# Reordering the start-up loads of a convolution and feed-forward kernel: weights by need, an ungated weight load, and one input held back

**The chip, the cores and the metric.** The kernel runs on one core of a Trainium2 chip. Times are device microseconds of that core, as medians of several executions of one build. The kernel before took 700.02 us when the prediction was made (three runs, 699.57 to 701.13).

## The reference, cut to what matters

```python
# x: [8, 4096, 192] f32, weight: [8 heads, 7] f32, w_in: [192, 2048], w_out: [2048, 192]
w   = softmax(weight, axis=-1)                    # 7 taps for each head of 24 channels
x_pad = concatenate([zeros(6 rows), x], axis=1)
y   = sum over k of w[h, k] * x_pad[:, s + k, h*24:(h+1)*24]    # causal depthwise convolution
h   = y.reshape(32768, 192) @ w_in
g   = maximum(0.01 * h, h)
out = g @ w_out                                   # [32768, 192] f32
```

## The kernel before

TensorE does both matrix products in bf16. VectorE does most of the convolution with one multiply and six multiply-adds for each chunk of 64 channels. ScalarE evicts the first product with the leaky ReLU. Two batch rows are worked on together, one in partitions 0 to 63 and one in 64 to 127, so `w_in` is needed in both halves of the partitions ("both rows"). The first blocks are cut in halves of 256 positions, to start early. A group is one such half. Group 0 has eight units; each unit is two 128-column tiles of `w_in`, twelve matmuls and one ScalarE activation of about 1 us.

Everything that the change touches is in the first 30 us. Four quarters of `w_in` are loaded with a cast on the way (f32 to bf16, from the GpSimd queue). Quarter 0 goes to both rows from HBM. Quarters 1 to 3 go to one row, and the sync queue copies them to the other on chip:

```python
    load_w_in(0, 0)
    load_w_in(0, 1)
    ...                                    # softmax, taps, first transposes
    for q in range(1, WQ):
        load_w_in(q, 0)                    # GpSimd queue, HBM -> row 0
    ...                                    # taps as diagonal matrices for TensorE
    for q in range(1, WQ):                 # sync queue, row 0 -> row 1
        nc.sync.dma_start(out=w_in[CH:128, :, fq[q]], in_=w_in[0:CH, :, fq[q]])
    load_first(2)                          # x of half 2, sync queue

    pjunk = const_pool.tile([1, 1], BF16)  # the gate: GpSimd reads the last w_in element
    nc.gpsimd.tensor_copy(out=pjunk, in_=w_in[0:1, NCH - 1, F - 1 : F])
    w_out = const_pool.tile([128, NFC, D], BF16)
    nc.gpsimd.dma_start(out=w_out, in_=moe_w_out.rearrange("(c p) d -> p c d", p=128))
    ...
    for job in conv_jobs(groups[0], range(NPEC, NCH)):
        job()
    load_first(3)                          # x of half 3, sync queue
```

In group 0 (i is the group, u the unit, j the step of two units):

```python
                mm1(grp, u)                                    # 12 matmuls and the activation
                if i == 0 and u == 3:
                    for job in pe_ahead: job()                 # convolution of half 1, on TensorE
                if i == 1 and u in (0, 2):
                    cast_first(3, u // 2, nc.scalar.copy)      # half 3 to bf16, on ScalarE
            ...
            if i == 0 and j == 3:                              # after unit 7
                ...
                for e in range(2): cast_first(2, e, nc.vector.tensor_copy)
                transpose_first(2)                             # on TensorE
                evac_first(2, nc.vector.tensor_copy, nc.vector.tensor_copy)
            ...
            if i == 1 and j == 1:
                transpose_first(3)
```

## Time and profile before

"Idle before" is the time in which TensorE stood still in front of a group of matmuls. The name behind it is what ended the wait. GpSimd's loads run on the software queue (q0 in the profile) and the sync engine's on the hardware queue (q1).

| Kernel before, profiled run | us |
|---|---|
| Span, TensorE busy | 698.4, 688.0 |
| Copies of w_in quarters 1, 2, 3: issued | 11.85, 12.86, 13.79 |
| The same: landed | 14.67, 15.66, 17.28 |
| w_out: issued, landed | 14.21, 25.45 |
| TensorE idle before unit 2 (copied w_in) | 0.91 |
| TensorE idle before half 2's transposes (x) | 1.63 |
| TensorE idle before the first use of w_out | 0.73 |
| VectorE starts half 2's convolution | 24.14 |
| TensorE meets VectorE at the first full block, and waits | 120.47, 0.62 |

### The profile page before, as it was taken

What the parts mean: (1) busy time and instruction counts of PE and PEld (TensorE: products, weight loads), DVE (VectorE), ACT (ScalarE), POOL (GpSimd) and SP (SyncE); (2) the same over time, 40 slices, a digit from 0 to 9 for tenths busy, and PEclk for the clock granted to TensorE, in tenths of its full rate; (3) what the DMA queues carried; (4) which work ended last, traced back from release to release, by engine and by line L of the source; (5) the groups of instructions that cost most, each with busy time, mean ns of one, the idle gap of its engine ahead of it and who ended that gap; (6) DMA issues with size and microseconds to landing.
All of it is one profiled execution on the core that took longest, in us unless ns stands there. A gap on an engine that the chain in (4) does not pass through costs nothing.

```text
span 698.4 us, 25999 instructions
## 1 busy us (share of the span) xinstructions
PE 688.0 (99%) x11756; PEld 610.6 (87%) x11756; DVE 542.8 (78%) x998; ACT 511.6 (73%) x571; POOL 142.3 (20%) x198
## 2 busy tenths in 40 slices
PE   8899999999999999999999999999999999999997
PEld 6799999678888888888888888888888888888887
DVE  7799999967777787777787777787777787777712
ACT  5778887977777777777777777777777777777770
POOL 4632220410222210222211222210222211000000
PEclk9999999999999999999999999999999999999999
DMA  7979544755565645556635556634556625122112
GB/s 149 131 91 101 83 71 81 80 77 79 73 74 86 85 66 75 77 74 86 86 65 81 73 74 84 88 69 74 75 74 84 89 63 77 54 52 60 45 36 70
DMA packets 184848, 54.39 MB, mean 78 GB/s; under 512 B 148384, under 2 KB 184736, under 8 KB 184736
## 3 DMA queue, kind: packets, MB, share of 16 engines
q0 software_dynamic: 98144, 13.58, 28.8%
q1 hardware_dynamic: 86592, 39.15, 23.5%
q8 instruction: 92, 1.51, 0.9%
q14 instruction: 20, 0.16, 0.1%
HBM read 28.70 MB, written 25.17 MB: 77 GB/s over the span
## 4 chain that ended last, share of the span: by engine, by line
PE 82%; DVE 13%; DMA 2%; issue 1%; POOL 1%; SPq 0%; ACT 0%; POOLq 0%; ACTq 0%
PE po L385 42%; PE ph L365 40%; DVE yt L174 12%; DMA w_in<-in_moe_w_in_dram 1%; DMA x_nat<-in_x_dram 1%; DVE yt L168 1%; POOL w_in L231 0%; DVE xt L149 0%; POOL sel L220 0%; ACT g L372 0%; SPq L319 0%; SPq L110 0%; DVE x_bf L120 0%; PE ptr L135 0%; POOL sel L218 0%
## 5 line engine op out<-in xcount | busy, mean ns | idle before, releaser
L372 ACT ACTIVATE g<-ph 128x1024 bf16<-128x1024 f32 x512 | 496.5, 1021 | 165.1 <-PE ph L365 165.1
L174 DVE SCALAR_TENSOR_TENSOR yt<-xt,wk,yt 128x512 bf16<-128x512 bf16 (+1 forms) x648 | 442.6, 683 | 17.7
L385 PE MATMUL po<-w_out,g 64*128 64x192 bf16 (+1 forms) x8048 | 398.2, 243 | 0.7 <-DMA w_out<-in_moe_w_out_dram 0.7
L385 PEld LDWEIGHTS <-g 64*128 64x128 bf16 (+1 forms) x8048 | 372.5, 94 | 29.5 <-issue 1.1
L365 PE MATMUL ph<-yt,w_in 64*128 64x512 bf16 (+1 forms) x3552 | 392.4, 347 | 3.0 <-ACT g L372 0.9
L365 PEld LDWEIGHTS <-w_in 64*128 64x128 bf16 x3552 | 249.9, 94 | 48.2 <-issue 5.1
L79 POOL DMA_DIRECT2D x_bf<-in_x_dram x180 | 133.7, 768 | 421.5 <-DMA xt<-x_bf 418.9
L424 DVE COPY o_sb<-po 128x192 f32<-128x192 f32 x216 | 77.3, 358 | 127.0 <-PE po L385 124.7
L168 DVE TENSOR_SCALAR yt<-xt,wk 128x512 bf16<-128x512 bf16 (+1 forms) x108 | 38.2, 353 | 0.1
L424 ACT COPY o_sb<-po 128x192 f32<-128x192 f32 x40 | 13.0, 325 | 0.0
L193 PE MATMUL acc<-xt,diag 64*64 64x256 bf16 x84 | 5.5, 282 | 0.0
L244 PE MATMUL warm<-zero 128*128 128x256 bf16 x18 | 4.3, 400 | 1.1 <-DVE junk L210 1.1
L193 PEld LDWEIGHTS <-diag 64*64 64x64 bf16 x84 | 4.5, 112 | 1.0 <-issue 0.6
L120 DVE CAST x_bf<-x_nat 128x384 bf16<-128x384 f32 x3 | 1.3, 424 | 4.8 <-DMA x_nat<-in_x_dram 4.8
L120 ACT CAST x_bf<-x_nat 128x384 bf16<-128x384 f32 x5 | 2.5, 506 | 1.9 <-DMA x_nat<-in_x_dram 1.9
L244 PEld LDWEIGHTS <-zero 128*128 128x128 bf16 x18 | 2.0, 131 | 1.9 <-DVE junk L210 1.1
L135 PEld LDWEIGHTS <-x_bf 64*128 64x128 bf16 x48 | 1.1, 101 | 2.6 <-DVE x_bf L120 1.9
L231 POOL DMA_DIRECT2D w_in<-in_moe_w_in_dram x5 | 3.3, 657 | 0.0
L135 PE MATMUL ptr<-ident,x_bf 64*128 64x64 bf16 x48 | 1.6, 202 | 1.6 <-DVE x_bf L120 1.6
L149 DVE COPY xt<-ptr 128x384 bf16<-128x384 bf16 x7 | 2.2, 352 | 0.4 <-PE ptr L135 0.4
L328 ACT ACTIVATE yt<-acc,rsum 128x256 bf16<-128x256 f32 x2 | 0.9, 474 | 1.9 <-PE acc L193 1.8
L296 ACT ACTIVATE diag<-ident,wkl 128x64 bf16<-128x64 bf16 x7 | 1.9, 339 | 0.0
(31 smaller groups left out, 14.4 us busy)
## 6 DMA issues: line engine op xcount, KB each, us to landing
out_dram<-o_sb SPq DMA_DIRECT2D x128, 192.0 KB, 2.1
x_bf<-in_x_dram POOLq DMA_DIRECT2D x180, 64.0 KB, 3.2
x_nat<-in_x_dram SPq DMA_DIRECT2D x8, 192.0 KB, 5.5
xt<-x_bf SPq DMA_TRANSPOSE x90, 2.5
w_in<-in_moe_w_in_dram POOLq DMA_DIRECT2D x5, 192.0 KB, 7.5
w_out<-in_moe_w_out_dram POOLq DMA_DIRECT2D x1, 768.0 KB, 11.2
w_in<-w_in SPq DMA_DIRECT2D x3, 192.0 KB, 2.8
w<-in_weight_dram SPq DMA_DIRECT2D x1, 0.2 KB
```

The costliest lines, as they stand in the source:

```text
L79: nc.gpsimd.dma_start(out=t[:, c, :, e, :], in_=src[2 * rp + e, :, :, c * CH : (c + 1) * CH],)
L120: copy(out=x_bf[q // 2][:, :, h * HS : (h + 1) * HS, e, :], in_=x_nat[q][:, e, :, :].rearrange("p s (c k) -> p c s k", c=NCH),)
L135: nc.tensor.transpose(out=ts[i][:, s, c, :], in_=x_bf[q // 2][ps, c, (q % 2) * HS + s, :, :].rearrange("p e k -> p (e k)"), identity=ident ...
L168: lambda s=src, d=dst, c=c: nc.vector.tensor_scalar_mul(d, s, wk[:, c, 0:1])
L174: lambda s=src, d=dst, c=c, k=k: nc.vector.scalar_tensor_tensor(out=d, in0=s, scalar=wk[:, c, k : k + 1], in1=d, op0=mybir.AluOpType.mult, ...
L193: lambda k=k, p=p, a=a, e=e, ps=ps: nc.tensor.matmul(out=acc[ps, :T], lhsT=diag[c][ps, p, k, :], rhs=xt[0][ps, c, a : a + T], start=(k == ...
L231: nc.gpsimd.dma_start(out=w_in[e * CH : (e + 1) * CH, :, fq[q]], in_=moe_w_in[:, fq[q]].rearrange("(c p) f -> p c f", p=CH),)
L244: nc.tensor.matmul(out=wa[:, 0, 0:HT], lhsT=zero[:, 0:128], rhs=zero, start=True, stop=True)
L365: nc.tensor.matmul(out=ph[:, e, i * T : (i + 1) * T], lhsT=w_in[ps, c, f * 128 : (f + 1) * 128], rhs=y[ps, c, t0 : t0 + T], start=(c == 0) ...
L372: act = nc.scalar.activation(out=g[blk][:, nf * u : nf * (u + 1), :, t0 : t0 + T], in_=ph.rearrange("p e (i t) -> p i e t", i=nf), func=my ...
L385: ins = nc.tensor.matmul(out=po[m], lhsT=g[b][ps, fc, e, s * 128 : (s + 1) * 128], rhs=w_out[ps, fc, :], start=(rt != 1 and fc == 0), stop ...
L424: copy(out=o_sb[:, n % 2, :], in_=po.pop(n))
```

## The change

The intent is to have each load arrive in the order in which it is needed. It has three parts.

* **Order.** Both rows of the first two quarters come from HBM, and only quarters 2 and 3 are copied on chip.
* **Ungated.** `w_out` is issued without waiting for `w_in`.
* **Hold.** x of half 3 is not issued until unit 5 of group 0 has been activated. Its casts and transposes move two units later.

A fourth, small item comes with it: the transposes of half 1 move behind both start-up convolutions, and two warming matmuls go.

```diff
-    def load_first(q):
+    def load_first(q, after=None):
 ...
+            if after is not None and e == 0:
+                tc.add_manual_dep(ins.ins, after.ins.name, ...)     # cut
 ...
-    for q in range(1, WQ):
+    load_w_in(1, 0)
+    load_w_in(1, 1)
+    for q in range(2, WQ):
         load_w_in(q, 0)
 ...
-    for q in range(1, WQ):
+    for q in range(2, WQ):
         nc.sync.dma_start(out=w_in[CH:128, :, fq[q]], in_=w_in[0:CH, :, fq[q]])
     load_first(2)
-
-    pjunk = const_pool.tile([1, 1], BF16)
-    nc.gpsimd.tensor_copy(out=pjunk, in_=w_in[0:1, NCH - 1, F - 1 : F])
     nc.gpsimd.dma_start(out=w_out, in_=moe_w_out.rearrange("(c p) d -> p c d", p=128))
 ...
-    load_first(3)
 ...                                       # transposes of half 1 after both convolutions
-                mm1(grp, u)
+                act = mm1(grp, u)
 ...
-                if i == 1 and u in (0, 2):
-                    cast_first(3, u // 2, nc.scalar.copy)
+                if i == 0 and u == 5:
+                    load_first(3, act)
+                if i == 1 and u in (4, 5):
+                    cast_first(3, u - 4, nc.scalar.copy)
 ...
-            if i == 1 and j == 1:
+            if i == 1 and j == 2:
                 transpose_first(3)
```

## The prediction

> **What bounds the kernel now.** I read the page first, then the chain that ended last, then the timeline of TensorE over the first 30 us, and last the DMA queues over short windows. From the page:
>
> ```profile
> PE 688.0 (99%) x11756; PEld 610.6 (87%) x11756; DVE 542.8 (78%) x998; ACT 511.6 (73%) x571; POOL 142.3 (20%) x198
> ...
> PE 82%; DVE 13%; DMA 2%; issue 1%; POOL 1%; SPq 0%; ACT 0%; POOLq 0%; ACTq 0%
> ```
>
> TensorE is busy for 688.0 of 698.4 us. The change only reorders loads at the start and adds no arithmetic, so all it can touch is part of the 10.4 us in which TensorE stands still. The whole of it would be 1.5% of the span. What can be won is decided by the chain, here its early part (start us, length us, what):
>
> ```profile
> 5.53 8.25 DMA w_in<-in_moe_w_in_dram
> ...
> 13.79 0.59 SPq L319
> ...
> 15.08 7.51 DMA x_nat<-in_x_dram
> ...
> 22.62 0.44 DVE x_bf L120
> ...
> 23.10 0.39 PE ptr L135 x12
> 23.50 0.62 DVE xt L149 x2
> ...
> 24.14 0.55 DVE yt L168
> ```
>
> The last w_in load lands at 13.78, the sync queue issues the third on-chip copy, then x of half 2. Its second part takes 7.51 us to land, is cast, transposed and evicted, and at 24.14 VectorE starts the convolution of half 2. From there the chain is VectorE alone until it hands over:
>
> ```profile
> 119.66 0.76 DVE yt L174
> ...
> 120.47 1.04 PE ph L365 x8
> ```
>
> So there are two clocks in the start. VectorE runs without a wait from 24.14 to 120.4. TensorE runs without one from 25.49 to 119.85, and there waits 0.62 us for VectorE. The end therefore moves by the smaller of two amounts: how much earlier VectorE starts half 2, and how much earlier TensorE gets into its steady flow plus 0.62. After 124 us TensorE has no wait longer than the issue gaps, so what is won by then is kept.
>
> TensorE in the start (the idle time before a group and its releaser in brackets):
>
> ```profile
> 11.70 1.38 PE L365 MATMUL ph<-yt,w_in 64*128 64x256 bf16 x22 [0.35 <-ACT yt L328]
> 13.53 0.27 PE L365 MATMUL ph<-yt,w_in 64*128 64x256 bf16 x1 [0.46 <-ACT g L372]
> 14.71 1.48 PE L365 MATMUL ph<-yt,w_in 64*128 64x256 bf16 x23 [0.91 <-DMA w_in<-w_in]
> 16.12 1.72 PE L193 MATMUL acc<-xt,diag 64*64 64x256 bf16 x28
> ...
> 19.72 1.75 PE L365 MATMUL ph<-yt,w_in 64*128 64x256 bf16 x24 [0.46 <-ACT g L372]
> 23.10 0.35 PE L135 MATMUL ptr<-ident,x_bf 64*128 64x64 bf16 x12 [1.63 <-DVE x_bf L120]
> ...
> 25.49 1.31 PE L385 MATMUL po<-w_out,g 64*128 64x192 bf16 x14 [0.73 <-DMA w_out<-in_moe_w_out_dram]
> ```
>
> The three DMA waits are what the change aims at: 0.91 us for the copied rows of w_in's second quarter, 1.63 for x of half 2, 0.73 for w_out. Together they are 3.3 us.
>
> **What the Trainium skill says.** "DMA: Bandwidth & Descriptors", section "Queues, rings and completion order", says that each DMA engine alternates between the queues it has work for, a packet at a time. That would give the sync queue its turn beside w_out. The trace agrees only late. Two windows of the DMA view, 18 to 20 us and then 21 to 23 us (packets, MB, share):
>
> ```profile
> q0 software_dynamic: 773, 0.30, 128.6%
> q1 hardware_dynamic: 68, 0.05, 10.3%
> ```
> ```profile
> q0 software_dynamic: 456, 0.17, 69.8%
> q1 hardware_dynamic: 416, 0.30, 61.3%
> ```
>
> In the first 3 us of w_out (from 17.0) x_nat on q1 nearly starves; from about 20.5 the two share about evenly, some 210 packets per us each. "Issuing engines are not separate DMA queues" on the same page says that all DMAs run on the same 16 engines; the starving shows that. "SBUF — State Buffer", section "SBUF: two separate sides", says that GpSimd and the faster modes of VectorE hold one port pair exclusively. The trace fits, on VectorE:
>
> ```profile
> 11.34 0.28 DVE L168 TENSOR_SCALAR yt<-xt,wk 128x256 bf16<-128x256 bf16 x1
> ...
> 14.66 0.80 DVE L168 TENSOR_SCALAR yt<-xt,wk 128x256 bf16<-128x256 bf16 x1
> ```
>
> The second one ended at 15.46, just after GpSimd's 1.22 us of w_out issue (14.21 to 15.43).
>
> **The change part by part.**
> (1) Second quarter of w_in. The five w_in loads are issued from 2.90 at 0.63 us each; the sync queue's waits put the landings of loads 3, 4 and 5 at 11.84, 12.86 and 13.78, so one lands about every 0.95 us. The new order has six: both rows of quarters 0 and 1, then one row of 2 and of 3. Quarter 1 is then whole at load 4, 12.9, where the copy landed at 14.67. But load 5 (quarter 2) comes at 13.8 and load 6 (quarter 3) at 14.7, each 0.95 later than now.
> (2) w_out. GpSimd no longer waits until 13.83. It issues the sixth load to 6.8, multiplies diag for 1.39 to 8.2, and issues w_out to 9.4. On one queue it flows behind w_in from about 13.3, instead of from 17.0. Its 2048 packets run alone at 390 per us until the copies start at about 15.3 (800 packets), and the rest at about 220: done near 20.8, against 25.4. First use is near 23, so the 0.73 wait goes. The price is that the copies and x of half 2 now run beside it.
> (3) The copies. Two, issued at 13.8 and 14.7. They took 2.8 us from issue to landing when alone and 3.5 for the third. At half the rate I take 3.8 to 4.5: quarter 2 at 17.6, quarter 3 at 19.2.
> (4) x of half 2 is issued at 15.4 and 15.9 (now 14.58 and 15.08). 512 packets of the sync queue follow the copies' 384; at about 200 per us and from 15.3 on that is 4.5 us with w_out, plus up to 1.5 for the slowest engine: second part down at 21.3, against 22.60. Half 3's 512 packets, in between now, are gone from here.
> (5) TensorE. The two warming matmuls and the transposes of half 1 leave the place between the two convolutions, so the second runs from 8.8 to 10.5 rather than 9.41 to 11.13, and ScalarE evicts it at 11.0 instead of 11.6. Work of group 0: units 0 and 1 end near 12.5 (13.1 now), units 2 and 3 start at 13.0 with quarter 1 and end at 14.4 (16.1), the convolution of half 1 runs to 16.1 (17.8). Then units 4 and 5 wait for quarter 2 until 17.6: a new wait of 1.5 us that eats most of this lead. They end at 19.0, ScalarE (0.97 us a unit) frees their buffers at 19.3 and 20.3, units 6 and 7 end at 21.0 (21.47).
> (6) So x of half 2 decides: 21.3, plus the cast to 21.75, transposes to 22.15, evictions to 22.8. VectorE starts half 2 at 22.8 rather than 24.14: 1.35 us earlier. TensorE's flow starts at 22.15 instead of 23.29 and without the 0.73: 1.9 us earlier, and the 0.62 on top. The smaller is 1.35.
> (7) Half 3 held until unit 5's activation (20.3): issued from 20.3, data from 22. The reads for block 2, issued after unit 7's activation near 22, push it aside only from 23.7. Its casts move two units later, to about 28, so I expect no wait.
> Sum: 700.0 - 1.35 = 698.6 us.
>
> **The rivals.** (a) All three waits go and nothing replaces them: TensorE ends group 0 near 20.2 and half 2's x is down by 20. VectorE would start near 21.8, a gain of 2.4, 697.6 us. For it: DMA has idle room around 12 to 13 us (28% share in the trace), which w_out would fill. Against it: the queue is near full from 15 to 23 anyway.
> (b) w_out starves the copies as it starves x_nat now (68 packets in 2 us). Quarter 2 would land at 19.5 or later, units 6 and 7 end at 22.8, VectorE starts at 24: a gain of 0.2 or a loss of up to 1, 699.8 to 701. For it: the first 3 us of w_out in the trace. Against it: output stores issued at 35 us, in the middle of a long flow on q0, land in 4.1 us, against 2.1 in the median, which is a halving and no starving.
> (c) The earlier GpSimd work (multiply and w_out issue, 6.8 to 9.4) holds VectorE's first TENSOR_SCALAR at 6.7. It would end at up to 9.4 instead of 7.64, unit 0 at 13.1, group 0's first half 0.7 later than now. The wait for quarter 2 hides that: no change of the time.
> (d) Half 3's x comes too late, ScalarE stands at the cast and holds TensorE's buffers. Over 1.1 us of it would cost time.
>
> **Range and chances.** Between (a) and (b) lie 697.6 and 701; repeats of before spread over 1.6 us. I lean to a small gain, so 697.2 to 700.4. A change of 2% is 14 us, more than all of TensorE's idle time, so within 2% gets 0.98, and 0.01 each for the others.
>
> **What would show it right or wrong.** VectorE's first TENSOR_SCALAR after the half 2 eviction at 22.8 (step 6); TensorE's wait for w_out gone (2); a wait on the copied w_in of 1 to 2 us before unit 4 (3, 5); copies landing in 3.8 to 4.5 us; x of half 2 down at 21.3 (4); no wait at the casts of half 3 (7); TensorE still waiting for VectorE near 119. Wrong it would be if copies took above 6 us, if half 2's x landed after 22.6, or if VectorE met a new wait before 119, such as the transposes of half 3.

## The result, and the profile after

The changed kernel took **702.94 us** (median of four, 702.64 to 703.11) against 699.89 us for the kernel before in the same rounds. The ratio is 1.004, with a 95% interval of 1.0022 to 1.0057. Ratios here are the mean time of one kernel's runs over that of the other's of the same rounds, so not quite the ratio of the medians quoted. The change is 3 us slower, where 1.35 us faster had been predicted. It is within 2%, but outside the range.

The page after, TensorE's busy line and the chain's shares by engine:

```profile
PE 690.6 (99%) x11754; PEld 611.6 (87%) x11754; DVE 542.1 (77%) x998; ACT 511.7 (73%) x571; POOL 141.9 (20%) x198
...
PE 83%; DVE 10%; DMA 3%; POOL 1%; ACT 1%; issue 1%; POOLq 0%; ACTq 0%
```

TensorE does two matmuls fewer and is busy for 2.6 us longer. So the loss is not only waiting: some matmuls became slower. (A part of this lies before 12 us, where full clock came later in this run: from 5 to 12 us TensorE did 88 matmuls in 7.00 us of work, against 96 in 6.65 before. Point 6 of the section on the prediction comes back to it.) The chain between 12 and 28 us shows both:

```profile
13.74 6.85 DMA w_in<-w_in
...
20.64 2.75 PE ph L369 x23
...
23.41 2.98 ACT g L376 x3
```

The on-chip copy of quarter 2 now takes 6.85 us from issue to landing. Then 23 matmuls of units 4 and 5 take 2.75 us. In the kernel before, the same kind of 23 took 1.48 us (the prediction shows that line, at 14.71). TensorE's timeline, with the idle time in brackets:

```profile
17.43 0.28 PE L369 MATMUL ph<-yt,w_in 64*128 64x256 bf16 x1
20.64 4.68 PE L369 MATMUL ph<-yt,w_in 64*128 64x256 bf16 x47 [2.93 <-DMA w_in<-w_in]
25.13 0.35 PE L143 MATMUL ptr<-ident,x_bf 64*128 64x64 bf16 x12
```

The wait for the copy is 2.93 us. Here are the busy times by stretch for 17 to 20.5 and for 20.5 to 24 us. After the stretch and its length come the engines' busy times, and the last three columns are TensorE's granted clock, the DMA share and GB/s:

```profile
17.00:20.50 3.50, 0.71 (x11) 0.32 (x7) 2.65 (x6) 0.00 (x0) 0.00 (x0) 1.00 1.13 197
20.50:24.00 3.50, 3.37 (x33) 2.34 (x35) 0.85 (x2) 1.62 (x2) 0.00 (x0) 0.51 0.10 27
```

The granted clock is 0.51 just after the wait. The clock records of this run have one window of 3.41 us at half clock, from 20.52 to 23.93. The half-clock window begins about where the wait ends (20.64).

Why was the copy late? The DMA view from 15 to 17 us, and then from 17 to 20.6 us (queue, packets, MB, share of the 16 engines' time):

```profile
q0 software_dynamic: 940, 0.36, 151.4%
q1 hardware_dynamic: 52, 0.05, 7.8%
```
```profile
q1 hardware_dynamic: 791, 0.65, 100.5%
q0 software_dynamic: 137, 0.05, 11.9%
```

While w_out fills q0, the copies on q1 get 52 packets against 940. When w_out is nearly through, q1 gets everything. The landings agree: w_out at 20.35, the two copies at 20.59 and 21.35. Both copies had been issued at 13.74 and 14.76.

At the other end of the start, the handover from VectorE to TensorE has moved by 2.80 us, from 120.47 to 123.27:

```profile
122.46 0.76 DVE yt L182
...
123.27 1.04 PE ph L369 x8
```

Of these 2.80 us, 2.02 are there when VectorE starts half 2 (26.16 against 24.14). From there to the handover VectorE had no wait in the kernel before. Now it has two:

```profile
35.27 0.62 DVE L157 COPY xt<-ptr 128x384 bf16<-128x384 bf16 x2 [0.41 <-PE ptr L143]
...
47.78 0.29 DVE L176 TENSOR_SCALAR yt<-xt,wk 128x256 bf16<-128x256 bf16 x1 [0.50 <-DMA xt<-x_bf]
```

The first is the wait for the transposes of half 3, which the prediction had named among the signs that it is wrong. The second is for the transposing load of a later block.

### The profile page after: what moved, and what is told of

The parts are those of the page before. It is cut to its first block, busy times and chain, and to the rows that moved or that the text cites. A ratio compares the mean times of both kernels' runs of the same rounds, so it can differ in the third digit from the quotient of the medians.

```text
span 700.9 us, 25993 instructions
## 1 busy us (share of the span) xinstructions
PE 690.6 (99%) x11754; PEld 611.6 (87%) x11754; DVE 542.1 (77%) x998; ACT 511.7 (73%) x571; POOL 141.9 (20%) x198
## 4 chain that ended last, share of the span: by engine, by line
PE 83%; DVE 10%; DMA 3%; POOL 1%; ACT 1%; issue 1%; POOLq 0%; ACTq 0%
PE po L390 42%; PE ph L369 41%; DVE yt L182 9%; DMA w_in<-in_moe_w_in_dram 1%; DMA w_in<-w_in 1%; DVE yt L176 1%; ACT g L376 1%; POOL x_bf L79 1%; DMA x_bf<-in_x_dram 1%; DMA xt<-x_bf 1%; POOL w_in L239 0%; POOL sel L228 0%; ACT x_bf L128 0%; POOL sel L226 0%; DVE o_sb L429 0%
## 5 line engine op out<-in xcount | busy, mean ns | idle before, releaser
L176 DVE TENSOR_SCALAR yt<-xt,wk 128x512 bf16<-128x512 bf16 (+1 forms) x108 | 36.5, 338 | 0.6 <-DMA xt<-x_bf 0.5
L476 POOL COPY pjunk<-g 1x1 bf16<-1x1 bf16 x1 | 0.2, 176 | 17.5 <-ACT g L376 17.5
```

The lines of the kernel that those rows point to most:

```text
L176: lambda s=src, d=dst, c=c: nc.vector.tensor_scalar_mul(d, s, wk[:, c, 0:1])
```

## The experiments

Each kernel was correct, and each was timed in five rounds against the kernel before on the same chip. (For e13 and e14, eleven of the twelve runs of before are earlier, so their ratios are weaker.) I began with two theories. **T1**: w_out, now in front, shuts the sync queue's copies out of the DMA engines. **T2**: the hold is the cost, since half 3 is cast late. Two more came up: **T3**, the new order itself, and **C**, a wait that TensorE pays for twice because its clock falls after it (with **D**, that it does not). The summary comes first. "Half clock" is what the clock records of the profiled run show between the warm-up and 40 us. The wait is TensorE's longest between 12 and 40 us.

| Run | Order, ungated, hold | First copy: issued, landed | w_out landed | Longest wait | Half clock, us | Median, us | Ratio to before (95%) |
|---|---|---|---|---|---|---|---|
| before | no, no, no | 11.85, 14.67 | 25.45 | 1.63 | none | 699.89 | |
| after | yes, yes, yes | 13.74, 20.59 | 20.35 | 2.93 | 3.41 | 702.94 | 1.0040 (1.0022 to 1.0057) |
| e1_ungate | no, yes, no | 11.52, 18.47 | 22.37 | 3.74 | 6.83 | 705.12 | 1.0060 (1.0046 to 1.0075) |
| e2_order | yes, no, no | 13.76, 16.68 | 27.90 | 3.60 | 10.24 | 702.56 | 1.0032 (1.0012 to 1.0052) |
| e3_hold | no, no, yes | 11.09, 14.81 | 23.37 | 1.37 | none | 700.14 | 0.9998 (0.9982 to 1.0013) |
| e4_after_gated | yes, no, yes | 13.88, 16.70 | 26.48 | 3.46 | 10.24 | 704.45 | 1.0045 (1.0025 to 1.0065) |
| e5_after_nohold | yes, yes, no | 14.06, 20.67 | 20.29 | 3.94 | 3.41 | 702.00 | 1.0009 (0.9985 to 1.0032) |
| e6_after_warm | after + filler | 14.26, 20.91 | 20.40 | 0.87 | none | 701.14 | 0.9996 (0.9975 to 1.0018) |
| e8_gated_warm | e4 + filler | 13.68, 16.48 | 25.21 | 0.87 | none | 700.41 | 0.9986 (0.9965 to 1.0007) |
| e9_after_again | yes, yes, yes | 13.57, 20.29 | 20.05 | 2.44 | 3.41 | 702.71 | 1.0033 (1.0017 to 1.0049) |
| e10_nohold_warm | e5 + filler | 13.99, 20.65 | 20.01 | 0.69 | none | 700.44 | 0.9996 (0.9983 to 1.0010) |
| e11_half_wout | after, w_out in halves | 13.84, 18.66 | 17.85, 25.41 | 2.19 | none | 700.09 | 0.9991 (0.9977 to 1.0005) |
| e14_copies_kept | e7 with copies | 14.29, 22.58 | 22.09 | 5.55 | 6.83 | 703.93 | 1.0024 (0.9998 to 1.0051) |
| e7_one_queue | one queue | no copies | 23.17 | 0.46 | none | 696.69 | 0.9931 (0.9909 to 0.9953) |
| e12_early_transpose | e7, transposes earlier | no copies | 21.79 | 0.89 | none | 697.02 | 0.9947 (0.9933 to 0.9960) |
| e13_x_on_sync | e7, x on sync queue | no copies | 22.41 | 0.51 | none | 698.25 | 0.9957 (0.9933 to 0.9980) |

One caution on the comparison. The kernel before itself spreads from 699.2 to 704.5 us, and the spread goes with its granted clock. Its runs with a mean clock of 0.999 or more have medians of 699.98, 700.56 and 700.35 us (e1 to e4, e5 to e8, e9 to e12). Those at 0.998 or less lie between 700.2 and 704.5. I call the first kind full-clock runs of before, and give the distance to them where the ratio alone would mislead.

**e1_ungate: only the gate of w_out is taken away**

```diff
-    nc.gpsimd.tensor_copy(out=pjunk, in_=w_in[0:1, NCH - 1, F - 1 : F])
```

> The kernel before with one thing changed: w_out is issued without the wait for w_in. Theory T1 (w_out, flowing behind w_in on the software queue from about 12.5 us, shuts the on-chip w_in copies out of the DMA engines until it is nearly through): all three copies land near 19 to 20 us instead of 14.7 to 17.3, TensorE stands about 5 us before unit 2 of group 0, its clock drops to half for a window of 3.4 us, and the time is 703 to 707 us. Theory T2 (the loss comes from half 3's x, held back and cast late; w_out is harmless): the wait for w_out (0.73 us) is gone and the time is 699 to 700 us.

Measured: 705.12 us. The three copies landed at 18.47, 20.20 and 21.23, that is 7 to 7.5 us after their issue instead of 2.8 to 3.5. TensorE waited 3.74 us before unit 2, and its clock was halved for 6.83 us. This is what T1 said. T2 said 699 to 700. Taken alone, the ungating is worse than the whole change. It should be noted that the copies here landed before w_out was wholly through (22.37).

**e2_order: only the new order of w_in**

```diff
-    for q in range(1, WQ):
+    load_w_in(1, 0)
+    load_w_in(1, 1)
+    for q in range(2, WQ):
         load_w_in(q, 0)
 ...
-    for q in range(1, WQ):                       # the copies
+    for q in range(2, WQ):
```

> The kernel before with one thing changed: both rows of w_in's second quarter come from HBM, and only two quarters are copied on chip; w_out stays gated, half 3 is not held. T1 and T2 both expect no harm: copies land in under 3.5 us each, the 0.91 us wait before unit 2 goes. x of half 2 is issued about 1 us later than before and meets w_out, so VectorE starts half 2 at 24 to 25 us: 699.5 to 701 us. Theory T3 (the order itself pushes quarters 2 and 3 too late): a wait of over 1 us before unit 4 or 6 and a time of 701.5 us or more.

Measured: 702.56 us, slower than all of the theories expected but T3, and for another reason than T3's. No copied quarter is waited for. The loss is x of half 2: issued at 16.94 and 17.45, it meets the gated w_out, and TensorE waits 3.60 us for it. Then it runs at half clock for 10.24 us in the profiled run, and VectorE stands 2.52 us for the transposes of half 3. This profiled run is the slowest of its six, and its sixth w_in load landed late (16.15, against 14.74 in the changed kernel), which held back the second copy and x behind it. The expectation had the meeting right and left out the clock. The six executions fall in two bunches, 701.6 to 701.7 at a mean clock of 0.998, and 703.5 to 705.2 at 0.993 to 0.994.

**e3_hold: only the hold of half 3.** The edit is the `load_first` and cast part of the diff above, on the kernel before.

> The kernel before with one thing changed: half 3's x is issued after unit 5 of group 0, and cast and transposed two units later. T1: half 2's x has no rival but w_out on its way, lands 0.5 to 1.5 us earlier, VectorE starts half 2 earlier, 698 to 700 us. T2: the casts of half 3 hold ScalarE and TensorE near 30 us by 0.5 to 1 us, VectorE waits for the transposes, and the time is 700.5 to 702 us.

Measured: 700.14 us, ratio 0.9998, the same as before. TensorE does wait for half 3's cast. Its timeline in this run:

```profile
32.09 0.55 PE L143 MATMUL ptr<-ident,x_bf 64*128 64x64 bf16 x12 [0.87 <-ACT x_bf L128]
```

The wait is 0.87 us in every profiled run of a kernel with the hold (after, e3, e4, e6, e8, e9, e11), and it does not come from the load: x had landed by 24.5 here. The second cast stands on ScalarE behind unit 5's activation, just in front of the transposes that need it. In e3 that was paid for, since w_out landed at 23.37 instead of 25.45 and the 0.73 us wait for it was gone. Half 3's x was out of its way, but w_out was also issued 1.0 us earlier in this run (13.17), and the two are not told apart. T2 is right on the wait and wrong that it is the loss.

**e4_after_gated: the changed kernel with the gate put back**

```diff
+    nc.gpsimd.tensor_copy(out=pjunk, in_=w_in[0:1, NCH - 1, F - 1 : F])
     nc.gpsimd.dma_start(out=w_out, in_=moe_w_out.rearrange("(c p) d -> p c d", p=128))
```

> The changed kernel with w_out gated again as before (its issue waits until the last row load of w_in has landed). T1: the two copies land in 2.8 to 3.5 us, by 17.7, no wait before unit 4, no clock drop; most of the 3 us loss goes, and the time is 699 to 701 us. T2: the loss stays, 702 to 703 us.

Measured: 704.45 us, no gain at all. The copies did what T1 said: 2.8 and 3.3 us from issue to landing, and no wait before unit 4. But now x of half 2, on the same sync queue, comes under w_out instead. TensorE waits 3.46 us for it, and is at half clock for 10.24 us. Behind that, VectorE stands 4.30 us for the transposes of half 3. So putting the gate back only exchanges which load of the sync queue is late. T1 as I had put it was incomplete: it is not only the copies that w_out delays. x's second part took 7.3 us, while its first part, issued 0.5 us earlier, still took 3.1.

**e5_after_nohold: the changed kernel without the hold**

```diff
-                if i == 0 and u == 5:
-                    load_first(3, act)
-                if i == 1 and u in (4, 5):
-                    cast_first(3, u - 4, nc.scalar.copy)
+                if i == 1 and u in (0, 2):
+                    cast_first(3, u // 2, nc.scalar.copy)
     # and load_first(3), transpose_first(3) back in their places
```

> The changed kernel with half 3's x issued, cast and transposed where the kernel before does it. T1 (w_out ahead of the copies): the copies still land at 20 to 21.5 us, the wait before unit 4 is still about 3 us, the clock still falls to half; half 3's x trails half 2's and half 2's is no earlier: 702 to 704 us. T2 (the hold is the cost): 700 to 701 us.

Measured: 702.00 us, which is 1.4 us above the full-clock runs of before (700.56). The ratio, 1.0009, looks milder because four of the eleven runs of before had a lower clock. The copy is as late as in the changed kernel (20.67), and the wait (3.94 us) and the half clock remain. The hold is not the main loss.

The stretches in the clock records last whole multiples of 3.41 us, so the clock is set by windows of that length, and here the wait lies across two of them. These two windows and the one after (columns as in the stretches shown for the changed kernel: after the length comes TensorE's busy time, and the clock is third from the end):

```profile
15.19:18.60 3.41, 1.58 (x27) 1.19 (x23) 3.19 (x8) 0.78 (x1) 0.00 (x0) 1.00 1.46 211
18.60:22.01 3.41, 1.29 (x23) 1.09 (x24) 0.32 (x2) 0.43 (x1) 0.00 (x0) 1.00 1.09 236
22.02:25.43 3.41, 3.01 (x37) 2.26 (x35) 0.79 (x2) 2.52 (x3) 0.00 (x0) 0.50 0.10 32
```

After a window with 1.58 us of work the clock stayed full. After one with 1.29 us it was halved. The last section counts this over all runs.

**e6_after_warm: the changed kernel with 28 matmuls on zeros before unit 4**

```diff
                 if i == 0 and u == 3:
                     for job in pe_ahead: job()
+                    keep = psum_o.tile([128, HT], FP32, name="keep", tag="po")
+                    for _ in range(28):
+                        nc.tensor.matmul(out=keep, lhsT=zero[:, 0:128], rhs=zero, start=True, stop=True)
```

> The changed kernel with 28 matmuls on zeros put in front of unit 4 of group 0, so that TensorE has something to do for the 3 us in which it waits for the copy. Theory C (a wait of about 3 us costs twice, since an idle TensorE is given half its clock in the next window of 3.41 us): copies land as late as before, but no half-speed window follows, units 4 and 5 take 1.4 instead of 2.75 us, and the time falls by 1 to 2.5 us, to 700.5 to 702 us. Rival D (the clock falls for another reason, or the half-speed window is hidden behind ScalarE): 702.5 to 703.5 us.

Measured: 701.14 us, as C says, against 702.94 and 702.71 for the changed kernel (in other calls; 0.6 us above the full-clock runs of before here, against 2.4 in e9's call). TensorE's timeline, and the stretch that had the clock of 0.51 in the changed kernel:

```profile
16.98 3.23 PE L463 MATMUL keep<-zero 128*128 128x256 bf16 x28
...
20.95 1.48 PE L369 MATMUL ph<-yt,w_in 64*128 64x256 bf16 x23 [0.54 <-DMA w_in<-w_in]
```
```profile
20.50:24.00 3.50, 2.51 (x39) 1.92 (x41) 0.85 (x2) 2.18 (x3) 0.00 (x0) 1.00 0.24 58
```

The copy was even later than in the changed kernel (20.91). The useless matmuls fill the wait, the clock stays at 1.00, and the 23 matmuls behind them take 1.48 us instead of 2.75. Nothing else was changed, so the half clock comes from the idle time.

**e8_gated_warm: the same filler before half 2's transposes, in e4**

> The changed kernel with w_out gated (e4), plus 28 matmuls on zeros in front of half 2's transposes, where e4 waited 3.46 us for x and then ran 10.24 us at half clock. C: no half-speed window, 4 us less time in that stretch for TensorE, so 2 to 4 us faster than e4 in the same state, 700 to 702.5 us. D: no change from e4, 702.3 to 706 us.

Measured: 700.41 us against e4's 704.45 (two chips; every one of its runs was at a clock of 0.999 or more, while e4's were at 0.992 to 0.997). Columns as above, for the stretch in which e4 was slow, e4 and then e8:

```profile
23.00:33.00 10.00, 8.82 (x83) 7.06 (x84) 8.38 (x20) 3.67 (x4) 8.29 (x12) 0.51 1.47 132
```
```profile
23.00:33.00 10.00, 8.97 (x163) 8.11 (x161) 8.59 (x20) 6.54 (x9) 8.12 (x11) 1.00 1.44 129
```

For the same busy time, 8.8 and 9.0 us, TensorE gets 83 matmuls done at half clock and 163 at full clock. Busy time alone hides this; the count and the clock column show it.

**e9_after_again: the changed kernel beside the next three**

> The changed kernel once more, so that it stands beside the next three on one chip: 702 to 704 us, ratio to before 1.001 to 1.005, a half-speed window after the wait for the copy in most runs.

Measured: 702.71 us, ratio 1.0033; the result holds on another chip. The wait was 2.44 us, and the half-speed window came.

**e10_nohold_warm: e5 with the filler of e6**

> The changed kernel without the hold (e5) and with the 28 matmuls on zeros of e6: what is left of the change is order and ungated w_out, at full clock. If the three causes add up (late copies about +1.3 us, clock about +1.5, hold about +0.5): 700 to 701.2 us, no half-speed window, no 0.87 us wait of TensorE for half 3's cast. If the hold costs nothing: the same as e6, 701 to 701.5.

Measured: 700.44 us, 0.1 above the full-clock runs of before (700.35). With the clock kept and the hold gone, no cost or gain of the order and the ungating together can be told from the spread of the runs (699.55 to 701.33). The copy landed at 20.65, TensorE's two late units came after a wait filled with zeros, and the wait for w_out was gone in exchange.

**e11_half_wout: w_out in two loads, the second after the last copy**

```diff
-    nc.gpsimd.dma_start(out=w_out, in_=moe_w_out.rearrange("(c p) d -> p c d", p=128))
+    pjunk = const_pool.tile([1, 1], BF16)
+    w_out_src = moe_w_out.rearrange("(c p) d -> p c d", p=128)
+    nc.gpsimd.dma_start(out=w_out[:, 0 : NFC // 2], in_=w_out_src[:, 0 : NFC // 2])
+    nc.gpsimd.tensor_copy(out=pjunk, in_=w_in[CH : CH + 1, NCH - 1, F - 1 : F])
+    nc.gpsimd.dma_start(out=w_out[:, NFC // 2 :], in_=w_out_src[:, NFC // 2 :])
```

> The changed kernel with w_out in two loads: the first half right away, the second only when the last copy has landed. T1 (a copy lands when the backlog of the software queue in front of it is through): half the backlog, so copies land near 17.5 and 18.5 us instead of 20.6 and 21.4, the wait before unit 4 is under 0.8 us, no half-speed window, 699.5 to 701.5 us. Rival (copies are slow for another reason, such as the second rows' own traffic): copies at 20 us or later, 702 us or more.

Measured: 700.09 us. The copies landed at 18.66 and 19.45, the first between the expected 17.5 and the 20.3 to 20.9 of the whole w_out: half the backlog, and about 2 us of the delay gone. The sixth w_in load was late in this run (16.19 instead of 14.7), which held back the second copy's issue. The wait was 2.19 us, not under 0.8, so my size was off; yet no half-speed window followed.

**e7_one_queue: all loads in order of need on the one software queue**

```diff
     for q in range(2, WQ):
-        load_w_in(q, 0)
+        for e in range(2):
+            load_w_in(q, e)
 ...
-    for q in range(2, WQ):
-        nc.sync.dma_start(out=w_in[CH:128, :, fq[q]], in_=w_in[0:CH, :, fq[q]])
-    load_first(2)
+    load_first(2, queue=nc.gpsimd)
     nc.gpsimd.dma_start(out=w_out, in_=moe_w_out.rearrange("(c p) d -> p c d", p=128))
+    load_first(3, queue=nc.gpsimd)
     # and the hold taken out, as in e5
```

> The changed kernel without copies and without the hold: all eight w_in loads, then x of half 2, then w_out, then x of half 3, on the one software queue, where the order of issue is the order of service. If T1 is right (what hurts is two queues, of which the software one is served first): quarter 2 of w_in is whole by 15, quarter 3 by 17, x of half 2 by 19.5, w_out by 24 us; no wait of TensorE above 1.5 us after unit 0, no half-speed window, VectorE starts half 2 near 22: 697 to 699.5 us. If the DMA engines are simply too slow for the sum of the loads: a new wait of 2 us or more for one of them and 700 us or more.

Measured: **696.69 us** (695.74 to 697.59), ratio 0.9931. This beats both kernels: 3.9 us below the full-clock runs of before (700.56). The loads landed in the order of issue: quarter 2 whole at 15.2, quarter 3 at 18.3, x of half 2 at 19.2, w_out at 23.2, x of half 3 at 24.3. TensorE's timeline:

```profile
19.49 1.75 PE L361 MATMUL ph<-yt,w_in 64*128 64x256 bf16 x24 [0.46 <-ACT g L368]
21.06 0.36 PE L135 MATMUL ptr<-ident,x_bf 64*128 64x64 bf16 x12
21.44 1.75 PE L361 MATMUL ph<-yt,w_in 64*128 64x256 bf16 x24
23.21 1.31 PE L382 MATMUL po<-w_out,g 64*128 64x192 bf16 x14
```

There is no wait for a DMA in it. All six runs were at full clock, since there is no long idle stretch to lose it in. VectorE starts half 2 at 22.09, 2.05 us before the 24.14 of before, and the handover at the first full block is at 118.38 instead of 120.47.

**e12_early_transpose: e7 with half 2's transposes between units 6 and 7**

> The one-queue kernel (e7) with half 2's casts, transposes and evictions placed between units 6 and 7 instead of after unit 7. There VectorE waited 0.86 us for the transposes and TensorE 0.92 us for VectorE at the handover. If the start of half 2 on VectorE is what sets the end: 0.5 to 0.9 us faster than e7, 695.6 to 696.3 us. If not: the same as e7, 696.4 to 697.2.

Measured: 697.02 us. This is a miss. VectorE's evictions of half 2 ended about half a microsecond sooner than in e7 (started at 20.94 instead of 21.43), but the handover was at 118.55, not sooner. VectorE stood twice for transposes, 0.8 us in all between 21 and 118 us against 0.9 once in e7, and its multiplies took 338 ns on average against 322. The two ran on different chips, so a difference of 0.3 us between them is not told apart.

**e13_x_on_sync: e7 with half 2's x back on the sync queue, issued after unit 0**

> The one-queue kernel (e7) with half 2's x on the sync queue, issued when unit 0's activation is done (near 14 us). T1 (a load on the sync queue waits for the software queue's backlog): x of half 2 lands at 21 us or later, though it is issued near 14, against 19.2 in e7 and 17.9 in e12; TensorE waits over 1 us for it before half 2's transposes, and the time is 698 to 700.5 us, with a half-speed window in some runs. Rival (the gain of e7 came from dropping the copies alone): x lands by 19.5 and the time is 696.4 to 697.4 us.

Measured: 698.25 us, 1.6 above e7 on the same chip. It was run at another time. The x landed at 18.67 and 19.89, not at 21 or later. It took 5.9 and 6.7 us from issue, but unit 0 ended earlier than I had assumed, so it was issued at 12.75. It had no start on w_out: from 12.5 to 16 us the sync queue moved no packet, while the software queue moved 1010. But from 17 to 19 us the two shared evenly (424 packets to 434), long before w_out had landed (22.41). So a load on the sync queue does not always wait until the software queue's backlog is through, and T1 in that form is wrong. My number missed, in the direction of the rival. The profiled run's waits in this stretch are small (0.51 us at most). It was the fastest of its six, and e7's, with the same span of 695.8 us, was the slowest of its six. How much of e7's gain is owed to the queue of x is between nothing and 1.6 us, and stays open. The queue is not the only difference: the trace shows x in packets of 768 bytes on the sync queue, and of 3072 and 4608 bytes on the software queue.

**e14_copies_kept: e7 with quarters 2 and 3 copied by the sync queue again**

> The one-queue kernel (e7) with quarters 2 and 3 of w_in copied on chip by the sync queue again, x of half 2 and w_out staying on the software queue in front of them in time. T1: the copies are issued near 13.8 and 14.8 and land at 20 us or later, TensorE waits over 2 us before unit 4, the clock falls in most runs: 700 to 703 us. Rival (the order of x was what mattered): copies by 18, time 696.5 to 698.5 us.

Measured: 703.93 us, 7 us slower than e7 on the same chip. It was run at another time. The chain of this run, and TensorE's waits between 10 and 30 us (total, times, longest):

```profile
14.29 8.29 DMA w_in<-w_in
...
22.62 3.80 PE ph L362 x29
```
```profile
PE ph L362 <- DMA w_in<-w_in: 5.6, 1, 5.6
```

With w_out and x of both halves issued in front on the software queue, the copy takes 8.29 us and lands at 22.58, half a microsecond after w_out (22.09). The same two copies that take about 3 us under a gated w_out (e2, e4, e8) are what ruins an otherwise good order.

## Why the prediction was wrong, point by point

1. **Where the time is decided.** Right. The gain or loss is made before the handover near 120 us, and almost nothing is added after it: 577.9 us from there to the end before, 577.7 after.
2. **Order, step (1).** Right. Quarter 1 was whole at 12.72, loads 5 and 6 landed at 13.72 and 14.74; predicted 12.9, 13.8 and 14.7.
3. **w_out, step (2).** The number is right, the way to it is not. It landed at 20.35, predicted 20.8, and the 0.73 us wait is gone. But the step had w_out share the DMA engines with the copies from 15.3 on, at 220 packets per us. It ran at 470 (940 in 2 us) with the copies shut out, and ended in a thin tail (137 packets from 17 to 20.6). That the two come out alike is luck.
4. **The copies, step (3): the step that failed.** "At half the rate I take 3.8 to 4.5" was the mis-sized term: 6.85 and 6.59 us were measured. The prediction had shown both regimes of the two queues, near starving for the first 3 us of w_out and even sharing later, and chose the later one. The copies came in the first. The argument against rival (b), output stores that landed in 4.1 us in a long flow on q0, did not carry over. That flow was of reads of x which are issued one by one, every 0.8 us, and landed some 3 to 4 us after their issue, while w_out was one load of 2048 packets already queued. I had the mechanism on the list as rival (b), at 699.8 to 701 us, and gave it too little weight. Copies above 6 us were also one of the prediction's own signs that it is wrong.
5. **What a wait costs, missing from every step.** The wait for quarter 2 was put at 1.5 us, and it was 2.93. But even rival (b)'s 701 us was too low, because no step had a term for TensorE's clock. The wait was followed by 3.41 us at half clock. The filler without the hold (e5 to e10, distance to the full-clock runs of before 1.4 and 0.1 us) puts this at about 1.3 us, and with the hold (e9 to e6, 2.4 and 0.6) at about 1.8. This is the largest single term of the loss. The prediction did not draw on "TensorE: Matmul & The Clock Gate" of the Trainium skill, though its section "Part 1: The HAM clock gate (the "warmup" mystery)" names the free-running window of 3413 ns and half clock after an idle one. The clock records agree with that figure: 3.41, 6.83 and 10.24 us. They do not agree that the window before must be idle: TensorE was busy for 0.60 us of it here (last section).
6. **Step (5).** "The second [convolution] runs from 8.8 to 10.5" was wrong in this run, 9.72 to 11.69, again by the clock. TensorE reached full clock at 7.50 in the profiled run before and at 10.28 after. As the matmuls up to 8.8 us are the same in both, I take this for where the free-running window happened to lie and not for the change; over the 16 profiled runs the instant lies anywhere between 7.50 and 10.68. Rival (c), VectorE held by GpSimd's issues, did not come: its first multiply took 0.28 us.
7. **x of half 2, step (4) and (6).** Predicted down at 21.3 and deciding. Its first part landed at 21.69, and the cast of the second followed within VectorE's 0.95 us for both, so it was down by about 22.2: that part of the step held to a microsecond, again not in the way predicted (next to nothing moved on its queue until 16.5 us, and then nearly everything did). It did not decide: TensorE reached the transposes only at 25.13, after the late and slow units.
8. **The hold, step (7).** "I expect no wait" was wrong by 0.87 us, which rival (d) had named with the wrong reason. The load was in time, the place of the cast on ScalarE was not. VectorE then stood 0.41 us for the transposes of half 3 in after, e6 and e9, and not at all in e5 and e10, which have no hold. In the times the cost is not told apart from nothing: from e6 to e10 it would be 0.5 us (0.6 to 0.1 above the full-clock runs), but e8 has the hold too and is level with before (700.41 against 700.56), and so is e3.

Taken step by step from the full-clock runs of before: order and ungating, with the clock kept, 0.1 us (e10); the hold on top, 0.5 (e6); the half clock on top, 1.8 (e9). The sum, 2.4 us, is e9's distance by construction; the first pair of medians gave 3.0 us. The steps come from two chips, and the runs of one kernel spread by 1.5 us (e6) to 3.0 us (e9). Only the half clock's step, which e5 to e10 and e4 to e8 show as well, stands clear of that; the other two do not.

What stays open: why the software queue's backlog is served first, and for how long. The runs show that it is at first (52 packets to 940), that sharing can become even while the backlog is still there (kernel before, e13), and that halving the backlog takes about 2 us off the copy's delay, but not by what rule in the DMA engines.

## What to carry to other kernels

Put loads that compete for the DMA engines in order of need on one queue, and don't count on a second queue to overtake a large load that is already waiting. Here the whole of that change (no copies, x on the same queue, no hold) was worth about 4 us, and a gate only moved the damage from the weights to the input. Count a TensorE wait of about 2 us or more at start-up as possibly more than its length (in these runs the clock fell when 2.1 us or more of one 3.41 us window were idle), read the granted clock of the stretch behind it, and compare runs by their clock before explaining a microsecond. When a reordering is sized, take the rate of the stretch in which the load will actually run, not the rate once both queues have settled.

## What the Trainium skill lacked or had wrong

* "DMA: Bandwidth & Descriptors", section "Queues, rings and completion order": it says that an engine alternates between the queues it has work for, packet by packet. With one load of 2048 packets queued by GpSimd, the runs show 52 packets of the sync queue to 940 of the software queue in 2 us, and copies of 6.3 to 8.3 us instead of 2.8 to 3.7. Even sharing came only later (456 to 416 in 2 us, kernel before). The page does not tell of this first regime. It counts a packet as a batch of typically 9 to 17 descriptors, and no run shows whether the trace counts the same, so the rule itself need not be wrong.
* "TensorE: Matmul & The Clock Gate", section "HAM oscillation — how this bites in real kernels": its rule is no idle gaps above about 3.4 us. Here a wait of 2.44 us (e9) and one of 2.93 us (after) were each followed by 3.41 us at half clock, while 2.19 us (e11) and 1.63 us (before) were not. What sorts all 16 profiled runs is TensorE's busy time in the 3.41 us windows of the clock records. Each of the seven full-clock windows with 1.29 us of work or less was followed by half clock (after 0.60, e4 0.94, e9 0.98, e2 1.04, e1 1.26, e14 1.28, e5 1.29), and none with 1.58 us or more was (e5 1.58, before 1.78, e11 1.86). So a wait that falls across two windows can be longer and cost nothing, as in e11 (1.86 and 2.31 us of work). No run was made to test this, or where between 1.29 and 1.58 us the limit lies.
* The same page, Part 1, gives the warm-up instant a spread of about 0.5 us, though it also says that the number of slow matmuls at the start varies much from run to run. The profiled runs here reach full clock between 7.5 and 10.7 us with the same matmuls up to 8.8 us, which makes a run-to-run difference that can be taken for an effect of a change.
* No page tells that half clock can go on through a window in which TensorE is busy throughout. In e2 (27.54 to 30.95) and e4 (26.52 to 29.93) it was busy for all 3.41 us, and one more half-clock window followed; in after, e5 and e9 one window with 3.01 to 3.41 us of work was enough to end it. (The 6.83 us of e1 and e14 are another case: there the wait itself reached into the first half-clock window.)
